# The last block's router logits, cut into bfloat16 parts and set among the first expert products

## The chip, the cores and the metric

The kernel runs on one NeuronCore of a Trainium2 chip. The metric is the device time of one execution in microseconds; less is better. Before the change it was 520.13 us, the median of 3 runs (519.86 to 521.75).

## The reference, cut to what matters

Three layers follow each other: a local-plus-summary attention, a dense layer with an ELU, and a top-1 mixture of 8 experts on 1536 tokens of width 512. The change touches only the router of the last layer and what hangs on it:

```python
logits = x @ w_gate                      # [1536, 512] @ [512, 8]
e_idx = np.argmax(logits, axis=1)
probs = np.exp(logits - logits.max(-1, keepdims=True))
probs /= probs.sum(-1, keepdims=True) + 1e-09
gate_w = probs[np.arange(N), e_idx]
eom = 1.0 / (1.0 + np.exp(-(x @ w_output_gate)))
for e in range(E):
    mask = e_idx == e
    h = np.maximum(x[mask] @ w1[e], 0.0)
    out[mask] = gate_w[mask, None] * eom[mask, e, None] * (h @ w2[e])
```

Both gates stand side by side in one matrix of 16 columns (`wg`).

## The kernel before, in words

Tokens are worked on in four blocks (512, 256, 384 and 384 tokens). For each block the kernel computes attention, then the dense layer chunk by chunk; `mm_y` ends it, `out_y1` takes a tile of 128 tokens to SBUF (tile `m`) and stores it to DRAM (`mdram`). Then the tile is transposed on TensorE (`lg_turn`) and multiplied with the gates (`lg2`). Blocks 0 to 2 do this with three bfloat16 parts of the transposed tile (`mab` holds the two upper parts, `mc` the rest) against three parts of the gates (`wg3`, 48 columns), which `lg_parts` makes in four steps: ScalarE, VectorE, ScalarE, VectorE. Block 3 copies its three tiles (`mt`) and multiplies in float32 with 16 columns.

After block 3 comes the expert layer, in slots of 128 tokens of one expert. The first two slots (0 and 1) were chosen early, from the first nine tiles alone; all other slots need the routing of all twelve tiles. So after block 3's logits a chain runs, mostly on VectorE: `route_block` (argmax and counts), the count matmul and `route_a2` (which expert owns which slot), `route_gate_*` (weights), `route_b` and `places` (place of each token), the twelve matmuls of `invert`, and `lists`, which makes `gixL` (rows to gather), `sixL` (rows to scatter to) and `sclL` (weights). With `gixL`, POOL gathers the tokens of a slot from `mdram` (`x_load`, tile `xg`, an indirect DMA); TensorE transposes them (`x_T`), and ScalarE and VectorE split them into a high and a low part (`holdh`, `holdl`). Here slots 2, 3 and 4 are the first late ones. The gather of slot i+2 is issued when slot i has been transposed. `route_a3` makes `nxi`, the experts that come next; SP waits for it and then loads the next expert's weights (`load_next`, 4 MB into `wo`). Behind those loads, in the same queue, stand the loads of the small slots' weights (`w_direct`, tiles `w2q`, `w2p`).

While the chain runs, TensorE works on slots 0 and 1: 48 products of 128 x 512 in `mm1` (tile `h`) and 48 in `mm2` (tile `y`), with four groups of transposes between (`g_T`, tile `S`). "Product" below always means one of these.

The order of the last part is written by a small planner, `second`: each step has an engine, a cost from the table `COST` and the steps it needs, and the planner picks what can start first. Engines run their lists strictly in that order. `flag` loads a slot's expert number into a register of ScalarE and VectorE, and `renew` is a branch on it: if a slot's expert is that of the slot before, nothing is converted.

Of the kernel before, what the change touches and what calls it, by code (L numbers as in the profile page):

```python
# [70 lines left out]
PB, PX = 2, 3  # L71
LF, NL = KF - 2, KF - 2 + PB + PX
NY = 2 * (PB + PX)
COST = {'m': 0.685, 'mp': 0.907, 't': 0.43, 'a': 0.48, 'l': 0.6, 'o': 0.57, 'g': 1.04, 'hAct': 0.52, 'lat': 0.08, 'xg': 2.0, 'dma': 0.73, 'pc': 0.1, 'px': 0.3, 'pg': 0.4, 'pb': 0.0, 'tol': 0.05, 'if': 0.15}
START2 = dict(PE=1.9, Act=0.9, DVE=1.4, Pool=0.5)
PARTS = range(8), range(8, 12), range(12, 16)
SEQ = (2, 3, 4, 11, 5, 6, 12, 7, 8, 9, 10)
# [4 lines left out]
class Prog:  # L82
# [499 lines left out]

    def lg_parts(self, j, t):

        nc, T = self.nc, self.mT.pop((j, t))
        if j == NBLK - 1:
            mt = self.t2k.tile([128, 512], F32, tag="t2k", name="mt")
            (nc.vector.tensor_copy if t == 1 else nc.scalar.copy)(mt, T)
        else:
            ab, c, r = (self.stg.tile([128, n, 512], dt, tag="stg", name=nm) for n, dt, nm in ((2, BF16, "mab"), (1, BF16, "mc"), (1, F32, "mr")))  # L590
            mt = [ab[:, 0], ab[:, 1], c[:, 0]]
            nc.scalar.copy(mt[0], T)
            nc.vector.tensor_tensor(r[:, 0], T, mt[0], op=ALU.subtract)
            nc.scalar.copy(mt[1], r[:, 0])
            nc.vector.tensor_tensor(mt[2], r[:, 0], mt[1], op=ALU.subtract)
        self.mt[j, t] = mt

    def lg2(self, j, t):
        nc = self.nc
        mt = self.mt.pop((j, t))  # L600
        if j < NBLK - 1:
            L = (self.bank(self.psa, "S") if j == NBLK - 2 else self.bank(self.psy, "y"))[:, :48]
            for k in range(4):
                for i in range(3):
                    nc.tensor.matmul(L, lhsT=mt[i][:, k * 128:k * 128 + 128], rhs=self.wg3[:, k], start=(k == 0 and i == 0), stop=(k == 3 and i == 2))
            nc.vector.tensor_reduce(self.lg[:, U0[j] // 2 + t], L.rearrange("p (i n) -> p n i", i=3), axis=AX.X, op=ALU.add)
            return
        if t == 0:
            self.L3 = self.bank(self.psy, "y")
        for k in range(4):  # L610
            nc.tensor.matmul(self.L3[:, t * 16:t * 16 + 16], lhsT=mt[:, k * 128:k * 128 + 128], rhs=self.wg[:, k], start=(k == 0), stop=(k == 3))

    def lg3(self):
        n = TPB[-1]
        self.nc.vector.tensor_copy(self.lg[:, NTT - n:], self.L3[:, :16 * n].rearrange("p (t e) -> p t e", t=n))

    def part1(self):
        nc = self.nc
# [212 lines left out]
    def route_gate_e(self, j):  # L831
# [2 lines left out]
        self.nc.scalar.activation(den[:, 1], z, AF.Exp, scale=-1.0)  # L834
        self.gate[j] = ex, den

    def route_gate_b(self, j):
        nc, sm = self.nc, self.small
        n = TPB[j]
        ts = slice(U0[j] // 2, U0[j + 1] // 2)  # L840
        ex, den = self.gate[j]
        nc.vector.tensor_reduce(den[:, 0], ex, axis=AX.X, op=ALU.add)
        nc.vector.tensor_scalar(den[:, 0], den[:, 0], 1e-9, None, op0=ALU.add)
        nc.vector.tensor_scalar(den[:, 1], den[:, 1], 1.0, None, op0=ALU.add)
# [65 lines left out]
    def lists(self, key, ps, n):  # L910
        nc = self.nc
        tk = self.small("f_tk" + key, [6, n])
        nc.vector.tensor_copy(tk, ps.rearrange("p (v s) -> p v s", s=n))
        ix = self.small("f_ix", [NL])[:, :n]
        nc.vector.scalar_tensor_tensor(ix, tk[:, 1], 128.0, tk[:, 0], op0=ALU.mult, op1=ALU.add)
        gix = self.const.tile([128, n], U32, name="gix" + key)
        six = self.const.tile([128, n], U32, name="six" + key)
        scl = self.const.tile([128, n], F32, name="scl" + key)
        nc.vector.tensor_copy(gix, ix)
        o = self.small("f_o", [NL])[:, :n]  # L920
        nc.vector.tensor_scalar(o, tk[:, 5], -4096.0, 4096.0, op0=ALU.mult, op1=ALU.add)
# [369 lines left out]
    def second(self, seq, t, start=False):  # L1291
# [72 lines left out]
        if start:  # L1364
            J = NBLK - 1
            for i in range(TPB[J]):
                e, d = ("DVE", C["l"]) if i == 1 else ("Act", C["a"])
                mm("c", ("yl", i), C["m"], [], lambda i=i: self.mm_y1(J, NF - 1, i))
                op(("m", i), e, d, [("yl", i)], lambda i=i: self.out_y1(J, i))
                op(("md", i), "Pool", C["g"], [("m", i)], lambda i=i: self.store_m(nc.gpsimd, J, i))  # L1370
            for i in range(TPB[J]):
                e, d = ("DVE", C["l"]) if i == 1 else ("Act", C["a"])
                mm("c", ("lt", i), C["t"], [("m", i)], lambda i=i: self.lg_turn(J, i))
                op(("mt", i), e, d, [("lt", i)], lambda i=i: self.lg_parts(J, i))
            for i in range(TPB[J]):
                mm("c", ("lg", i), 0.84, [("mt", i)], lambda i=i: self.lg2(J, i))
            op(("lv",), "DVE", 0.12, [("lg", i) for i in range(TPB[J])], self.lg3)
            op(("rb",), "DVE", 1.62, [("lv",)], lambda: self.route_block(J))
            mm("c", ("cnt",), 0.05, [("rb",)], self.count)
            mm("c", ("rm",), 0.05, [("rb",)], lambda: self.rank_mm(TE, NTT, self.fin))  # L1380
            op(("left",), "DVE", 0.1, [("cnt",)], self.left)
            op(("ga",), "DVE", 0.3, [("rb",)], lambda: self.route_gate_a(J))
            op(("ge",), "Act", 0.25, [("ga",)], lambda: self.route_gate_e(J))
            op(("a2",), "DVE", 2.75, [("left",)], self.route_a2)
            op(("rk",), "DVE", 0.35, [("rm",)], lambda: self.rank_of(TE, NTT, self.fin))
            op(("gb",), "DVE", 0.6, [("ge",)], lambda: self.route_gate_b(J))
            op(("gc",), "Pool", 1.4, [("gb",)], lambda: self.route_gate_c(J))
            op(("a4",), "DVE", 1.05, [("a2",)], self.route_a4)
            op(("b1",), "DVE", 2.3, [("a4",), ("rk",)], self.route_b)
# [12 lines left out]

            for i in range(16):
                if i < WN:
                    done["w", chain[0], i] = 0.0
                    continue
                self.ew[0, i] = self.new_place(f"wi{i}")
                op(("h0", i), "Act", C["hAct"], [], lambda i=i: self.conv_hi("Act", 0, i, self.ew[0, i]))
                op(("w", 0, i), "DVE", C["l"], [("h0", i)], lambda i=i: self.last_w(i))
        else:  # L1410
            done["xg", 0] = C["xg"]
            for i in range(16):
                done["w", chain[0], i] = C["xg"]
            half = [(0.0, p) for i in range(8) for p in self.float_places(f"wi{i}")]
# [17 lines left out]
        while any(pe.values()) or fixed:  # L1432
# [152 lines left out]
```

## Time and profile before

| What | Value |
|---|---|
| Median of 3 runs | 520.13 us |
| Profiled execution's own time | 519.82 us |
| Its span (first to last instruction) | 518.0 us |
| TensorE busy | 508.6 us, 98% |
| VectorE, ScalarE, POOL busy | 65%, 59%, 11% |
| Mean granted TensorE clock | 0.994 of full |

TensorE's busy time is modelled, so waits show better in the places where two products stand further apart than usual. The span's parts: dense layer until about 339 us, logits of block 3 until 343.7 us, slots 0 and 1 until 371.2 us, then the late slots until 512 us and a tail for the last scatter.

### The profile page before, as it was taken

The page shows a single profiled execution, that of the slowest core. Times are in us where ns is not written, and L with a number is a line of the kernel's source. Part 1 is how long each engine was busy: PE and PEld are TensorE (multiplying, and loading weights), DVE is VectorE, ACT ScalarE, POOL GpSimd, SP SyncE. Part 2 cuts the span into 40 slices and gives each one's busy share as a digit, 9 for nine tenths or more (in the row PEclk, how much of TensorE's full clock was granted, in tenths as well). Part 3 has the DMA queues.
Part 4 walks back from the last instruction along what each step waited for, and adds up shares of the span by engine and source line. Part 5 has one row for each costly group of instructions (what it writes and reads, how often), then busy time and mean ns, then how long its engine had stood idle before and what let it go on. Part 6 is the DMA issues. An engine that isn't in the chain of part 4 may idle for free. (4 is left out here: it accounts for less than half of the span.)

```text
span 518.0 us, 9835 instructions
## 1 busy us (share of the span) xinstructions
PE 508.6 (98%) x3325; PEld 408.5 (79%) x3325; DVE 336.7 (65%) x945; ACT 305.0 (59%) x715; POOL 57.2 (11%) x103
## 2 busy tenths in 40 slices
PE   8999999999999999999999999999999999999995
PEld 6486778888988889888899898888788566576884
DVE  5999999999798768776557899658321011445510
ACT  3899999986777667656546556433232222556521
POOL 3510200001000000000000001013411111100001
PEclk9999999999999999999999999989999999999998
DMA  8999444561420221200001034210599899594501
GB/s 287 404 398 317 146 133 138 183 198 50 135 77 7 83 82 42 83 15 1 2 0 63 1 126 164 78 62 1 157 339 301 292 348 360 168 364 143 213 23 44
DMA packets 37131, 78.08 MB, mean 151 GB/s; under 512 B 3951, under 2 KB 9807, under 8 KB 37072
## 3 DMA queue, kind: packets, MB, share of 16 engines
q1 hardware_dynamic: 34752, 70.02, 39.7%
q0 software_dynamic: 2320, 7.34, 4.0%
q8 instruction: 28, 0.46, 0.4%
q14 instruction: 31, 0.25, 0.2%
HBM read 100.37 MB, written 6.55 MB: 206 GB/s over the span
## 5 line engine op out<-in xcount | busy, mean ns | idle before, releaser
L483 PE MATMUL h<-xh,wi 128*128 128x384 f32 (+2 forms) x528 | 141.8, 337 | 1.5 <-DVE elp L509 1.5
L544 PE MATMUL y<-wsp,gh 128*128 128x512 f32 x368 | 116.8, 399 | 0.0
L483 PEld LDWEIGHTS h<-xh,wi 128*128 128x128 f32 x528 | 93.9, 189 | 9.4 <-DVE elp L509 1.9
L483 PE MATMUL h<-xl,wi 128*128 128x384 f32 (+2 forms) x264 | 87.5, 332 | 0.0
L544 PEld LDWEIGHTS y<-wsp,gh 128*128 128x128 f32 x368 | 66.5, 188 | 12.1 <-issue 0.3
L544 PE MATMUL y<-wsp,gl 128*128 128x512 f32 x184 | 72.4, 393 | 0.0
L1228 DVE TENSOR_TENSOR holdl<-S,holdh 128x512 fp32r<-128x512 f32 x22 | 15.2, 690 | 73.2 <-ACT holdh L1224 55.1
L1196 PE MATMUL h<-w2s,holdh 128*128 128x512 f32 x176 | 61.1, 408 | 0.0
L1239 PE MATMUL y<-w2s,holdh 128*128 128x512 f32 x176 | 59.0, 398 | 0.0
L483 PEld LDWEIGHTS h<-xl,wi 128*128 128x128 f32 x264 | 49.9, 189 | 3.8 <-issue 0.5
L503 DVE SCALAR_TENSOR_TENSOR elt<-ele,elt 128x384 f32<-128x384 f32 (+2 forms) x64 | 35.5, 554 | 24.3 <-ACT ele L496 23.9
L175 ACT CAST wsp<-wo 128x512 fp32r<-128x512 f32 x62 | 38.0, 618 | 19.9 <-PE y L544 19.1
L179 DVE TENSOR_TENSOR wsp<-wo,wsp 128x512 fp32r<-128x512 f32 x62 | 42.6, 688 | 8.3 <-ACT wsp L175 8.2
L496 ACT ACTIVATE elt<-h 128x384 f32<-128x384 f32 (+2 forms) x64 | 31.2, 487 | 25.1 <-PE h L483 24.4
L519 ACT CAST gh<-elp 128x384 fp32r<-128x384 f32 (+2 forms) x62 | 31.5, 509 | 20.9 <-DVE elp L509 13.8
L544 PEld LDWEIGHTS y<-wsp,gl 128*128 128x128 f32 x184 | 34.6, 188 | 7.9 <-DVE gl L525 0.3
L525 DVE TENSOR_TENSOR gl<-elp,gh 128x384 fp32r<-128x384 f32 (+2 forms) x62 | 34.0, 549 | 10.2 <-ACT gh L519 9.9
L1196 PEld LDWEIGHTS h<-w2s,holdh 128*128 128x128 f32 x176 | 33.7, 191 | 8.2 <-issue 0.8
L354 ACT ACTIVATE e<-e,nb 128x120 f32<-128x120 f32 x88 | 33.6, 386 | 9.8 <-DVE nb L341 9.8
L1239 PEld LDWEIGHTS y<-w2s,holdh 128*128 128x128 f32 x176 | 33.1, 188 | 6.7
L1273 DVE TENSOR_TENSOR w2s<-wo,w2s 128x512 fp32r<-128x512 f32 x48 | 30.4, 686 | 10.5 <-PE y L1239 5.5
L509 DVE SCALAR_TENSOR_TENSOR elp<-elt,h 128x384 f32<-128x384 f32 (+2 forms) x64 | 35.1, 548 | 0.8
(291 smaller groups left out, 820.4 us busy)
## 6 DMA issues: line engine op xcount, KB each, us to landing
wo<-in_w SPq DMA_DIRECT2D x9, 2048.0 KB
wo<-in_w SPq DMA_DIRECT2D x18, 1024.0 KB
ri<-in_w_in SPq DMA_DIRECT2D x16, 512.0 KB
ro<-in_w_out SPq DMA_DIRECT2D x16, 512.0 KB
wo<-in_w SPq DMA_DIRECT2D x32, 256.0 KB
w2p<-in_w SPq DMA_DIRECT2D x32, 256.0 KB
w2q<-in_w SPq DMA_DIRECT2D x24, 256.0 KB
k<-in_kw SPq DMA_DIRECT2D x18, 192.0 KB
```

Of the source, the lines that this page charges most:

```text
L175: self.nc.scalar.copy(w[:, 0], self.w[c, 1].bitcast(F32))
L179: self.nc.vector.tensor_tensor(w[:, 1], self.w[c, 1].bitcast(F32), w[:, 0].bitcast(F32), op=ALU.subtract)
L354: nc.scalar.activation(e[:, p], e[:, p], AF.Exp, bias=nb[:, p:p + 1], scale=-1.0, accum_out=sm[:, p:p + 1])
L483: nc.tensor.matmul(h, lhsT=w[:, wl, k * 128:k * 128 + 128], rhs=x[:, k, a:b], start=(n == 0), stop=(n == 11))
L496: self.nc.scalar.activation(self.te[j, c][i], self.h[j, c], AF.Exp if i else AF.Tanh, scale=1.0 if i else 0.5)
L503: nc.vector.scalar_tensor_tensor(t, e, 1.0, t, op0=ALU.add, op1=ALU.mult)
L509: nc.vector.scalar_tensor_tensor(p, t, 0.0, h, op0=ALU.min, op1=ALU.max)
L519: self.nc.scalar.copy(gh, p)
L525: self.nc.vector.tensor_tensor(gl, p, gh.bitcast(F32), op=ALU.subtract)
L544: nc.tensor.matmul(self.y[j][t], lhsT=gx[:, sl], rhs=wx, start=(c == 0 and n == 0), stop=(c == NF - 1 and n == len(ops) - 1))
L1196: nc.tensor.matmul(self.h[s, hf], lhsT=x[:, k], rhs=w, start=(n == 0), stop=(n == 11))
L1239: nc.tensor.matmul(self.y2[s], lhsT=g[:, ks], rhs=w, start=(i == 0 and n == 0), stop=(i == 7 and n == 2))
```

## The change

In block 3, tiles 0 and 1 are now cut into three bfloat16 parts as in the other blocks (in buffers of a former `x` tile: `mh`, `ml`); tile 2 stays in float32. The steps of the cutting are planned one by one (`lg_b`, `lg_c`, `lg_d`). The logits stand after the first six products, tile 2 first. Two conversions of slot 0's weights wait until the second tile `m` has been copied. Two small additions of the gate weights go from VectorE to POOL. The gathers no longer stand behind the making of `sixL` and `sclL` (`list_rest`), and `route_a3` now needs the lists and slot 1's last `holdl`, not slot 2's transposed tokens. In `COST` a gather of the first two late slots is given 3.1 us to land instead of 2.0.

```diff
-COST = {'m': 0.685, 'mp': 0.907, 't': 0.43, 'a': 0.48, 'l': 0.6, 'o': 0.57, 'g': 1.04, 'hAct': 0.52, 'lat': 0.08, 'xg': 2.0, 'dma': 0.73, 'pc': 0.1, 'px': 0.3, 'pg': 0.4, 'pb': 0.0, 'tol': 0.05, 'if': 0.15}
+COST = {'m': 0.685, 'mp': 0.907, 't': 0.43, 'a': 0.48, 'l': 0.6, 'o': 0.57, 'g': 1.04, 'hAct': 0.52, 'lat': 0.08, 'xg': 2.0, 'dma': 0.73, 'pc': 0.1, 'px': 0.3, 'pg': 0.4, 'pb': 0.0, 'tol': 0.05, 'if': 0.15, 'xf': 3.1}
...
     def lg_parts(self, j, t):
-        nc, T = self.nc, self.mT.pop((j, t))
+        if j == NBLK - 1 and t > 1:
+            self.mt[j, t] = [self.t2k.tile([128, 512], F32, tag="t2k", name="mt")], None
+            self.nc.scalar.copy(self.mt[j, t][0][0], self.mT.pop((j, t)))
+            return
         if j == NBLK - 1:
-            mt = self.t2k.tile([128, 512], F32, tag="t2k", name="mt")
-            (nc.vector.tensor_copy if t == 1 else nc.scalar.copy)(mt, T)
+            if t == 0:
+                n = TPB[j]
+                self.mab, self.mc = (self.xp.tile([128, n, 512], F32, tag=f"x{p}{j % 2}", name=f"m{p}").bitcast(BF16).rearrange("p t (i n) -> p t i n", i=2) for p in "hl")
+            mt = [self.mab[:, t, 0], self.mab[:, t, 1], self.mc[:, t, 0]]
+            r = self.t2k.tile([128, 512], F32, tag="t2k", name="mr")
...
+    def lg_b(self, j, t):
+        mt, r = self.mt[j, t]
+        self.nc.vector.tensor_tensor(r, self.mT.pop((j, t)), mt[0], op=ALU.subtract)
+
+    def lg_c(self, j, t):
+        mt, r = self.mt[j, t]
+        self.nc.scalar.copy(mt[1], r)
+
+    def lg_d(self, j, t):
+        mt, r = self.mt[j, t]
+        self.nc.vector.tensor_tensor(mt[2], r, mt[1], op=ALU.subtract)
...
+    def lg3a(self):
+        self.nc.vector.tensor_copy(self.lg[:, NTT - 1], self.L3[:, 96:112])
     def lg3(self):
-        n = TPB[-1]
-        self.nc.vector.tensor_copy(self.lg[:, NTT - n:], self.L3[:, :16 * n].rearrange("p (t e) -> p t e", t=n))
+        self.nc.vector.tensor_reduce(self.lg[:, NTT - 3:NTT - 1], self.L3[:, :96].rearrange("p (t i e) -> p t e i", t=2, i=3), axis=AX.X, op=ALU.add)
...
+    def route_gate_d(self, j):
+        den = self.gate[j][1]
+        eng = self.nc.gpsimd if j == NBLK - 1 else self.nc.vector
+        eng.tensor_scalar(den[:, 0], den[:, 0], 1e-9, None, op0=ALU.add)
+        eng.tensor_scalar(den[:, 1], den[:, 1], 1.0, None, op0=ALU.add)
...
         nc.vector.tensor_copy(gix, ix)
+        if key == "L":
+            self.rest = lambda: self.list_rest(tk, ix, n, six, scl)
+        else:
+            self.list_rest(tk, ix, n, six, scl)
+        return gix, six, scl
...
-            op(("li",), "DVE", 1.4, [("inv",)], lambda: setattr(self, "L_", self.lists("L", self.slots_of(), NL)))
+            op(("li",), "DVE", 0.65, [("inv",)], lambda: setattr(self, "L_", self.lists("L", self.slots_of(), NL)))
             for i in (2, 3):
                 op(("xg", i), "Pool", C["g"], [("li",)], lambda i=i: self.x_load(seq[i]))
+            op(("lj",), "DVE", 0.9, [("on", "xg", 2)], lambda: self.rest())
             op(("f", 2), "Act", 0.46, [("li",)], lambda: self.flag(2))
-            op(("a3",), "DVE", 1.6, [("xl", 2)], self.route_a3)
+            op(("a3",), "DVE", 1.6, [("lj",), ("gl", 1, 1)], self.route_a3)
...
-                op(("w", 0, i), "DVE", C["l"], [("h0", i)], lambda i=i: self.last_w(i))
+                op(("w", 0, i), "DVE", C["l"], [("h0", i)] + ([("m", 1)] if i > 13 else []), lambda i=i: self.last_w(i))
```

TensorE, from the transposes of block 3 on, before the change:

```order
L580 MATMUL T<-c_162,m 128x128 x4
L580 MATMUL S<-c_162,m 128x128 x4
L580 MATMUL y<-c_162,m 128x128 x4
L611 MATMUL y<-rc,mt 128x16 x12
L1196 MATMUL h<-w2s,holdh_4461 128x512
L1196 MATMUL h<-w2s,holdl_4462 128x512
```

The same place after the change (`c` is the identity, `rc` and `wg` the gates in float32 and in parts):

```order
L580 MATMUL y<-c_162,m 128x128 x4
L1239 MATMUL h<-w2s,holdh_4461 128x512
L1239 MATMUL h<-w2s,holdl_4462 128x512
L1239 MATMUL h<-w2s,holdh_4461 128x512 x2
L1239 MATMUL h<-w2s,holdl_4462 128x512
L1239 MATMUL h<-w2s,holdh_4461 128x512
L627 MATMUL y<-rc,mt 128x16 x4
L633 LDWEIGHTS mh
L633 MATMUL y<-wg_1005,mh 128x48
```

Six products now stand before the logits; of the twelve float32 matmuls four are left, and 24 short ones with 48 columns follow.

VectorE, the rows up to `nxi`, before the change (the first row is the split of slot 2's tokens, the others are `route_a3`):

```order
L1180 TENSOR_TENSOR holdl_4462<-T,holdh_4461 128x512
L1028 TENSOR_SCALAR f_e_4976<-f_en 128x8
L1031 TENSOR_TENSOR mask<-rc,f_e_4976 128x72
L1032 SCALAR_TENSOR_TENSOR mask<-mask,f_e_4976 128x72
L1034 TENSOR_REDUCE f_to<-mask 128x9
L1035 TENSOR_TENSOR mask<-f_to,f_e_4976 128x72
L1036 TENSOR_REDUCE f_to<-mask 128x9
L1038 TENSOR_SCALAR nxi<-f_to,e_1029 128x9
L1039 TENSOR_SCALAR nxi<-nxi 128x9
```

The same step after the change:

```order
L1071 TENSOR_SCALAR f_e_4978<-f_en 128x8
L1074 TENSOR_TENSOR mask<-rc,f_e_4978 128x72
L1075 SCALAR_TENSOR_TENSOR mask<-mask,f_e_4978 128x72
L1077 TENSOR_REDUCE f_to<-mask 128x9
L1078 TENSOR_TENSOR mask<-f_to,f_e_4978 128x72
L1079 TENSOR_REDUCE f_to<-mask 128x9
L1081 TENSOR_SCALAR nxi<-f_to,e_1029 128x9
L1082 TENSOR_SCALAR nxi<-nxi 128x9
L1223 TENSOR_TENSOR holdl_4462<-T,holdh_4461 128x512
```

`nxi` now stands ahead of the split of slot 2's tokens and no longer behind it.

TensorE where the late slots' tokens are transposed, before the change (slots 3 and 4, then slot 2's first products):

```order
L1171 MATMUL T<-identr,xg 128x128 x4
L1239 MATMUL y<-w2s,holdh_4838 128x512
L1239 MATMUL y<-w2s,holdl_4839 128x512
L1239 MATMUL y<-w2s,holdh_4838 128x512 x2
L1239 MATMUL y<-w2s,holdl_4839 128x512
L1239 MATMUL y<-w2s,holdh_4838 128x512 x2
L1239 MATMUL y<-w2s,holdl_4839 128x512
L1239 MATMUL y<-w2s,holdh_4838 128x512
L1171 MATMUL T<-identr,xg 128x128 x4
L1282 UNCONDITIONAL_BRANCH
L1196 MATMUL h<-w2s,holdh_4461 128x512
```

And after it:

```order
L1214 MATMUL T<-identr,xg 128x128 x4
L1325 UNCONDITIONAL_BRANCH
L1239 MATMUL h<-w2s,holdh_4461 128x512
L1239 MATMUL h<-w2s,holdl_4462 128x512
L1239 MATMUL h<-w2s,holdh_4461 128x512 x2
L1239 MATMUL h<-w2s,holdl_4462 128x512
L1239 MATMUL h<-w2s,holdh_4461 128x512 x2
L1239 MATMUL h<-w2s,holdl_4462 128x512
L1239 MATMUL h<-w2s,holdh_4461 128x512
L1325 UNCONDITIONAL_BRANCH x2
L1214 MATMUL T<-identr,xg 128x128 x4
L1239 MATMUL h<-w2s,holdh_4461 128x512
```

The transposes of slots 2, 3 and 4 each stand nine products later than before, with the same nine between one and the next; slot 4's now come after nine of slot 2's own products.

## Rows read from the trace of the kernel before

**Rows 1.** Part 1 of the page: busy time, share, instructions of each engine.

```profile
PE 508.6 (98%) x3325; PEld 408.5 (79%) x3325; DVE 336.7 (65%) x945; ACT 305.0 (59%) x715; POOL 57.2 (11%) x103
```

**Rows 2.** Windows of one us: busy per engine, then clock, DMA share, GB/s.

```profile
344.00:345.00 1.00, 1.00 (x4) 0.77 (x4) 0.86 (x5) 0.22 (x1) 0.00 (x0) 0.69 0.04 12
345.00:346.00 1.00, 1.00 (x4) 0.76 (x3) 0.83 (x6) 0.00 (x0) 0.00 (x0) 0.50 0.00 0
346.00:347.00 1.00, 1.00 (x4) 0.56 (x2) 0.11 (x1) 0.21 (x1) 0.00 (x0) 0.50 0.00 0
347.00:348.00 1.00, 1.00 (x6) 0.77 (x6) 0.45 (x4) 0.00 (x0) 0.00 (x0) 0.61 0.00 0
```

**Rows 3.** Timeline 341 to 344: start, length, engine, line, tiles, shapes [idle before].

```profile
341.14 2.75 PE L611 MATMUL y<-rc,mt 128*128 128x16 f32 x24
...
343.74 0.48 PE L1196 MATMUL h<-w2s,holdh 128*128 128x512 f32 x1
```

**Rows 4.** Timeline of TensorE, 144 to 146: block 0's logits by parts.

```profile
144.92 0.22 PE L605 MATMUL y<-wg,mab 128*128 128x48 bf16 x2
...
145.23 0.36 PE L483 MATMUL h<-xh,wi 128*128 128x256 f32 x1
```

**Rows 5.** Groups by line, 136 to 222: busy us, mean ns | idle before.

```profile
L593 DVE TENSOR_TENSOR mr<-y,mab 128x512 f32<-128x512 f32 x6 | 4.1, 686 | 0.0
...
L594 ACT CAST mab<-mr 128x512 bf16<-128x512 f32 x6 | 3.7, 622 | 1.9 <-DVE mr L593 1.9
```

**Rows 6.** Timeline 347 to 363: the routing chain, from the counts to the gather.

```profile
347.52 0.16 DVE L996 SCALAR_TENSOR_TENSOR e_c<-taken,y 128x8 f32<-128x8 f32 x1 [1.41 <-PE y L880]
...
350.90 0.18 DVE L842 TENSOR_REDUCE r_den<-r_ex 128x3 f32<-128x24 f32 x1 [0.19 <-ACTq L1282]
...
359.95 0.50 PEld L908 LDWEIGHTS <-A 128*128 128x128 bf16 x12 [0.26 <-DVE v L902]
...
361.12 0.17 DVE L919 CAST gixL<-f_ix 128x14 uint32<-128x14 f32 x1
...
361.90 0.17 DVE L925 TENSOR_TENSOR sclL<-sclL,f_tkL 128x14 f32<-128x14 f32 x1
...
362.06 1.09 POOL L1157 DMA_INDIRECT xg<-mdram,gixL  x1 [4.05 <-PE y L1239]
```

**Rows 7.** Timeline 361.9 to 371.5: products, gathers, transposes of slots 2 to 4.

```profile
361.95 0.39 PE L1239 MATMUL y<-w2s,holdl 128*128 128x512 f32 x1
...
362.64 0.39 PE L1239 MATMUL y<-w2s,holdl 128*128 128x512 f32 x1
...
365.60 0.39 PE L1239 MATMUL y<-w2s,holdh 128*128 128x512 f32 x1
...
366.23 0.53 PE L1171 MATMUL T<-identr,xg 128*128 128x128 f32 x4 [0.24 <-DMA xg<-mdram,gixL]
...
367.03 0.98 POOL L1157 DMA_INDIRECT xg<-mdram,gixL  x1 [0.38 <-DMA xg<-mdram,gixL]
...
367.42 0.69 DVE L1180 TENSOR_TENSOR holdl<-T,holdh 128x512 fp32r<-128x512 f32 x1 [4.48 <-ACT holdh L1176]
...
369.82 0.17 DVE L1039 TENSOR_SCALAR nxi<-nxi 128x9 int32<-128x9 int32 x1
...
371.01 13.88 SPq L1499 DMA_DIRECT2D wo<-in_w  x5
...
371.16 0.46 PE L1171 MATMUL T<-identr,xg 128*128 128x128 f32 x4
...
371.42 0.33 DVE L1065 TENSOR_TENSOR mask<-rc,f_T 128x160 f32<-128x160 f32 x1 [0.83 <-DVEq L1282]
```

**Rows 8.** DMA issues: gathers issued at 367.03, 371.89, 380.24; last, us to landing.

```profile
xg<-mdram,gixL POOLq DMA_INDIRECT x1, 3.4
...
xg<-mdram,gixL POOLq DMA_INDIRECT x1, 7.8
...
xg<-mdram,gixL POOLq DMA_INDIRECT x1, 6.9
```

**Rows 9.** Waits of TensorE's weight loads from 340 on: total us, times, longest.

```profile
PEld h L1205 <- DMA w2p<-in_w: 0.6, 2, 0.3
```

More of the change, by code (lines that the diff above doesn't have):

```diff
@@ L591, in lg_parts @@
             mt = [ab[:, 0], ab[:, 1], c[:, 0]]
[L592 to L596, printed above, removed]
+            r = r[:, 0]
+        self.mt[j, t] = mt, r
+        self.nc.scalar.copy(mt[0], self.mT[j, t])
+        if j < NBLK - 1:
+            self.lg_b(j, t)
+            self.lg_c(j, t)
+            self.lg_d(j, t)
@@ L598, in lg2 @@
+    def lg_b(self, j, t):
[7 more added lines that the diff above has]
+        self.nc.vector.tensor_tensor(mt[2], r, mt[1], op=ALU.subtract)
     def lg2(self, j, t):
         nc = self.nc
-        mt = self.mt.pop((j, t))
+        mt = self.mt.pop((j, t))[0]
+        if j == NBLK - 1:
+            if t == 2:
+                self.L3 = self.bank(self.psy, "y")
+            L = self.L3[:, t * 48:t * 48 + 48]
+            if t > 1:
+                for k in range(4):
+                    nc.tensor.matmul(L[:, :16], lhsT=mt[0][:, k * 128:k * 128 + 128], rhs=self.wg[:, k], start=(k == 0), stop=(k == 3))
+                return
+        else:
+            L = (self.bank(self.psa, "S") if j == NBLK - 2 else self.bank(self.psy, "y"))[:, :48]
+        for k in range(4):
+            for i in range(3):
+                nc.tensor.matmul(L, lhsT=mt[i][:, k * 128:k * 128 + 128], rhs=self.wg3[:, k], start=(k == 0 and i == 0), stop=(k == 3 and i == 2))
@@ L601, in lg2 @@
         if j < NBLK - 1:
[L602 to L605, printed above, removed]
             nc.vector.tensor_reduce(self.lg[:, U0[j] // 2 + t], L.rearrange("p (i n) -> p n i", i=3), axis=AX.X, op=ALU.add)
-            return
-        if t == 0:
-            self.L3 = self.bank(self.psy, "y")
@@ L610, in lg2 @@
-        for k in range(4):
-            nc.tensor.matmul(self.L3[:, t * 16:t * 16 + 16], lhsT=mt[:, k * 128:k * 128 + 128], rhs=self.wg[:, k], start=(k == 0), stop=(k == 3))
+    def lg3a(self):
+        self.nc.vector.tensor_copy(self.lg[:, NTT - 1], self.L3[:, 96:112])
     def lg3(self):
-        n = TPB[-1]
-        self.nc.vector.tensor_copy(self.lg[:, NTT - n:], self.L3[:, :16 * n].rearrange("p (t e) -> p t e", t=n))
+        self.nc.vector.tensor_reduce(self.lg[:, NTT - 3:NTT - 1], self.L3[:, :96].rearrange("p (t i e) -> p t e i", t=2, i=3), axis=AX.X, op=ALU.add)
@@ L835, in route_gate_e, with route_gate_z @@
         self.gate[j] = ex, den
+    def route_gate_z(self, j):
+        ex, den = self.gate[j]
+        self.nc.vector.tensor_reduce(den[:, 0], ex, axis=AX.X, op=ALU.add)
+    def route_gate_d(self, j):
[3 more added lines that the diff above has]
+        eng.tensor_scalar(den[:, 1], den[:, 1], 1.0, None, op0=ALU.add)
     def route_gate_b(self, j):
@@ L840, in route_gate_b @@
         ts = slice(U0[j] // 2, U0[j + 1] // 2)
[L841 to L844, printed above, removed]
+        if j < NBLK - 1:
+            self.route_gate_z(j)
+            self.route_gate_d(j)
+        den = self.gate[j][1]
         nc.vector.reciprocal(den, den)
@@ L919, in lists, with list_rest @@
         nc.vector.tensor_copy(gix, ix)
+        if key == "L":
+            self.rest = lambda: self.list_rest(tk, ix, n, six, scl)
+        else:
+            self.list_rest(tk, ix, n, six, scl)
+        return gix, six, scl
+    def list_rest(self, tk, ix, n, six, scl):
+        nc = self.nc
         o = self.small("f_o", [NL])[:, :n]
@@ L925, in lists @@
         nc.vector.tensor_tensor(scl, scl, tk[:, 4], op=ALU.add)
-        return gix, six, scl
     def route_early(self):
@@ L1373, in second @@
                 mm("c", ("lt", i), C["t"], [("m", i)], lambda i=i: self.lg_turn(J, i))
[L1374 to L1377, printed above, removed]
+                op(("ma", i), "Act", C["a"], [("lt", i)], lambda i=i: self.lg_parts(J, i))
+                if i == 2:
+                    continue
+                op(("mb", i), "DVE", C["l"], [("ma", i)], lambda i=i: self.lg_b(J, i))
+                op(("mc", i), "Act", C["a"], [("mb", i)], lambda i=i: self.lg_c(J, i))
+                op(("mt", i), "DVE", C["l"], [("mc", i)], lambda i=i: self.lg_d(J, i))
+            mm("c", ("lg", 2), 0.9, [("ma", 2)], lambda: self.lg2(J, 2))
+            for i in range(2):
+                mm("c", ("lg", i), 0.34, [("mt", i)], lambda i=i: self.lg2(J, i))
+            op(("la",), "DVE", 0.2, [("lg", 2)], self.lg3a)
+            op(("lv",), "DVE", 0.25, [("lg", 0), ("lg", 1), ("la",)], self.lg3)
             op(("rb",), "DVE", 1.62, [("lv",)], lambda: self.route_block(J))
@@ L1385, in second @@
             op(("rk",), "DVE", 0.35, [("rm",)], lambda: self.rank_of(TE, NTT, self.fin))
-            op(("gb",), "DVE", 0.6, [("ge",)], lambda: self.route_gate_b(J))
+            op(("gz",), "DVE", 0.2, [("ge",)], lambda: self.route_gate_z(J))
+            op(("gd",), "Pool", 0.45, [("gz",)], lambda: self.route_gate_d(J))
+            op(("gb",), "DVE", 0.2, [("gd",)], lambda: self.route_gate_b(J))
             op(("gc",), "Pool", 1.4, [("gb",)], lambda: self.route_gate_c(J))
             op(("a4",), "DVE", 1.05, [("a2",)], self.route_a4)
-            op(("b1",), "DVE", 2.3, [("a4",), ("rk",)], self.route_b)
+            op(("b1",), "DVE", 2.3, [("a4",), ("rk",), ("gl", 0, 0)], self.route_b)
             op(("pp",), "Pool", 0.58 * (NTT - PD), [("b1",)], lambda: self.places(nc.gpsimd, PD, NTT))
@@ L1473, in second @@
                 o[4]()
-                done[o[0]] = end + (C["xg"] if o[0][0] == "xg" else 0.0)
+                done[o[0]] = end + ((C["xf"] if start and o[0][1] < 4 else C["xg"]) if o[0][0] == "xg" else 0.0)
+                done[("on",) + o[0]] = st
                 if o[0][0] == "ld":
```

## The prediction

> **What bounds the kernel now.** I read the page first: TensorE is busy for 98% of the span [rows 1], so a change counts only where it shortens TensorE's list, ends a wait of TensorE, or makes a new one. Then I read the granted clock in windows of one microsecond: over the whole span until TensorE's last product it falls only once, to its lower level (1.2 GHz), from about 344.4 to 347.8 [rows 2]. What stood just before are the 24 passes of block 3's float32 logits, 16 columns each [rows 3]. The missing shares of those four windows, 0.31 + 0.50 + 0.50 + 0.39, are 1.70 us lost. Then I followed the timeline of the routing chain to slot 2's tokens [rows 6, 7], because it sets when TensorE's next work is there. TensorE waits in it twice: for VectorE at the twelve matmuls of `invert` (0.26 us) [rows 6], and for the gather at slot 2's transposes. There the last product starts at 365.60, the transposes at 366.23; a product takes 0.23 us (three start within 0.69) [rows 7], so 0.40 us of the step is wait. From there on TensorE waits for next to nothing; the only transfer that it is seen waiting for is `w2p`, 0.6 us [rows 9].
>
> **The change, part by part.** Times are those of the profiled execution (span 518.0, own time 519.82, which is 0.31 under the median of 520.13).
>
> *Logits.* Before, they fill TensorE from 341.14 to 343.74, 2.60 us, 0.108 per pass [rows 3]. After, 8 passes (four matmuls of tile 2) are left, 0.87 us. The 24 short matmuls I price by block 0, where twelve of them stand between 144.92 and 145.23 [rows 4]: 0.31 us for twelve, 0.62 for 24. The parts of tile 1 are ready late: two conversions, then four subtractions of 0.69 and two casts of 0.62 [rows 5] end at about 343.8 by my count, and the last twelve matmuls could start at 343.7, so 0.1 us is waited. Sum 1.6 us instead of 2.6: **−1.0**. The six products set ahead cover the cutting; without them about 1.4 us of it would be bare.
>
> *The clock.* The 2.6 us of small work become 1.6 us with 1.4 us of full products ahead of them. No row of before shows this mixture, so the price lies between 0 (it falls as before) and −1.70 (it doesn't). The nearest row is that of block 0, where twelve such short matmuls lie between full products and the clock stays at its upper level; I take **−1.70**.
>
> *The chain.* The logits end 0.4 us later (344.1 for 343.7), but the count matmul, which stood behind nine slow products (VectorE waited 1.41 us for it [rows 6]), now stands 12 products of full speed behind the logits: 344.1 + 2.8 = 346.9, and VectorE goes on some 0.3 us later, at 347.2 instead of 347.52. The sum and the two additions of the gate weights (the first takes 0.18 at 350.90 [rows 6]) leave the path, about −0.5. So `invert` could start at 359.95 − 0.3 − 0.5 = 359.15. TensorE, 2.7 us ahead and with six more products (1.4 us) to do before it, gets there at 358.4 and waits 0.7 us where it waited 0.26: **+0.4**.
>
> *Lists and gather.* Before, the gather starts at 362.06, 0.77 us after `gixL` (361.12 + 0.17) and close to the end of `sclL` at 362.07 [rows 6]. If it waited for the later lists, it now comes up to 0.5 us sooner; if not, nothing changes. Either way it is issued by about 361.3 and lands 4.1 us later as before, at 365.4; slot 2's transposes, 9 products later in the list, come at 365.7. So the old wait goes: **−0.4**.
>
> Up to slot 2's first product that is −2.7: 368.4 instead of 371.16 (slot 4's transposes apart, which stood ahead of it).
>
> *The new wait.* `nxi` waited for the split of slot 2's tokens at 367.42 and was ready at 369.99; SP then issued 4 MB of weights from 371.01 [rows 7]. Now `nxi` follows the lists: `invert` at 359.15, then 1.34 to `gixL`, 0.78 for the later lists, one register load and one branch (two branches and a load took 0.83 [rows 7]; 0.6 here), a split of 0.69 and `route_a3`, 1.9 (368.11 to 369.99): about 364.5. SP issues 1.0 us later, at 365.5, 5.5 us earlier than before. The gather for slot 4 can't follow: it is issued 0.8 us after slot 2's transposes (367.03 − 366.23 [rows 7]), now 365.7 + 0.8 = 366.5, so 1.0 us *behind* the weights, where it was 4.0 us ahead. Gathers issued before the weights land after 3.4 us; the one issued 0.88 us behind them, at 371.89, took 7.8, and one in the middle of them 6.9 [rows 8]. TensorE takes slot 4's tokens 4.93 us after slot 2's (371.16 − 366.23 [rows 7]; the list has the same nine products between each), now at 370.6. A gather of 3.4 lands at 369.9, in time; one of 6.9 to 7.8 lands at 373.4 to 374.3, and TensorE, strictly in order, stands for 2.8 to 3.7 us. Behind these transposes stand all of slot 2's later products. Between 0 and 3.7 I take **+3.0**, near the lower of the two crowded rows, since less of the stream is under way by then.
>
> Here a page speaks for the change. The Trainium skill (DMA: Bandwidth & Descriptors, section Queues, rings and completion order) says that each DMA engine takes turns between the queues that have work, packet by packet, so a gather from POOL's queue would lose little to SP's loads. The rows of 6.9 and 7.8 beside 3.4 don't bear that out for this kernel; by that rule the wait would be near 0 and the sum near −3.2.
>
> *Earlier weights.* The small slots' weights stand in SP's queue behind those 4 MB and come about 5 us earlier, so the wait for `w2p` goes: **−0.5** of the 0.6, at best −0.6 and at worst 0.
>
> *Rest.* POOL's two additions (each some 0.2) end long before VectorE's reciprocal; the delayed conversions of slot 0 are needed by its second layer's end, ten microseconds later. Behind slot 4's transposes the list of TensorE is the same as before. These cost nothing.
>
> Sum: −1.0 − 1.7 + 0.4 − 0.4 + 3.0 − 0.5 = −0.2, that is 519.6 for the profiled execution, **519.8** on the median. Most of what the logits give is taken back 26 us later by one gather.
>
> **The rivals.**
> *The gather slips through.* It lands in 3.4 us, because `nxi` is later than I count (2 us would surely do) or because the queues take turns. Then the +3.0 is 0: 519.8 − 3.0 = 516.8. For it: the rows have nothing between a gather 4.0 us ahead of the weights, untouched, and one 0.88 us behind them, crowded, so the border may lie close. Against: the order counted above, with 1.0 us on the wrong side.
> *The standing TensorE loses its clock.* In the wait of some 3 us TensorE has nothing at all, and 2.6 us of small work were enough to end at the lower level before. If it falls once more at the same price, +1.7: 521.5, slower than before. It decides from a wait of about the length of that small work on, so only where the crowded gather takes 6.9 us or more. Against: half a product group still stands on either side. The Trainium skill (TensorE: Matmul & The Clock Gate, section HAM oscillation) says likewise that waits for a transfer between bursts of matmuls can return the engine to its lower clock; the trace of before has no such wait to show it.
> *The clock falls at the logits as before,* so that the short matmuls among the products don't do for the clock what I count on. TensorE loses 1.7 us, the count comes 1.35 us later, the wait at `invert` shrinks by 0.35 and all after it shifts by 1.35; the gather is as crowded as in the main case. 519.8 + 1.3 = 521.1.
>
> **How the numbers follow.** My forecast (gather crowded, clock kept) 0.45; the gather slips through 0.21; the second fall 0.20; the first fall stays 0.14. The likeliest time is 519.8, its own range 518.8 to 520.6. Over all cases I give 516.8 to 522.0. A difference of 0.5% (2.6 us) is about what a measurement of this kernel can tell from no change, so "faster" means under 517.5: nearly only the gather that slips through, 0.20 with a little from the main case. "Slower" means over 522.7: both falls together or a longer wait, 0.11. The rest, 0.69, is no change.
>
> **What would show it.** Right: four float32 matmuls and 24 short ones after six products, done by 344.2; a clock at its upper level from 344 to 348; `nxi` near 364.5 and SP's first load of weights near 365.5; the gather for slot 4 landing after 6 us or more; a gap of TensorE of about 3 us before slot 4's transposes; no wait for `w2p`. Wrong: a clock of 0.5 in 344 to 348 (logits), `nxi` after 366 or a gather of 3.4 us (no gap), or a clock of 0.5 shortly after 371 (second fall). If slot 2's first product comes later than 369.5, my count of the chain has failed.

## The result and the profile after

The changed kernel takes **525.24 us** (median of 5 runs, 525.09 to 525.40), the kernel before 520.13 (5 runs, 519.29 to 521.75): ratio 1.0091, 95% interval 1.0070 to 1.0112. It is slower by 0.9%; 519.8 was forecast, with a range up to 522.0.

The logits first. The timeline of TensorE answers to [rows 3], the one-us windows (busy per engine, then clock, DMA share, GB/s) to [rows 2]:

```profile
340.51 0.60 PE L580 MATMUL T<-c,m 128*128 128x128 f32 x4
...
343.23 0.96 PE L627 MATMUL y<-rc,mt 128*128 128x16 f32 x8
344.04 0.21 PE L633 MATMUL y<-wg,mh 128*128 128x48 bf16 x2
...
344.76 0.21 PE L633 MATMUL y<-wg,mh 128*128 128x48 bf16 x2 [0.26 <-DVE lg L638]
...
345.06 0.47 PE L1239 MATMUL h<-w2s,holdh 128*128 128x512 f32 x1
```

```profile
345.00:346.00 1.00, 1.00 (x13) 0.87 (x10) 0.64 (x4) 0.00 (x0) 0.00 (x0) 1.00 0.04 16
346.00:347.00 1.00, 1.00 (x7) 0.79 (x6) 0.85 (x5) 0.22 (x1) 0.00 (x0) 1.00 0.00 0
347.00:348.00 1.00, 1.00 (x9) 0.66 (x7) 0.61 (x4) 0.70 (x3) 0.20 (x1) 1.00 0.00 0
```

Logits by parts and the clock came as counted: no fall, and from block 3's first transposes to the next product 4.55 us, of which the six products take 1.37 (0.2275 each). That leaves 3.18 for 4.05 before (339.69 to 343.74).

Six microseconds later is a wait that the forecast doesn't have. TensorE and VectorE, timeline:

```profile
350.09 0.39 PE L1239 MATMUL h<-w2s,holdl 128*128 128x512 f32 x1
351.51 0.73 PE L1239 MATMUL h<-w2s,holdh 128*128 128x512 f32 x2 [1.04 <-DVEq L1325]
```

```profile
350.92 0.23 DVE L1061 TENSOR_SCALAR esi<-f_es,e 128x9 int32<-128x9 f32 x1
351.18 0.17 DVE L1062 TENSOR_SCALAR esi<-esi 128x9 int32<-128x9 int32 x1
351.55 0.19 DVE L881 RECIPROCAL r_den<-r_den 128x6 f32<-128x6 f32 x1 [0.19 <-DVEq L1325]
```

Line 1325 is the branch of `renew` for slot 1. VectorE comes to it only after all of `route_a2`, whose last operations make `esi`. Behind the branch VectorE would write the low part of slot 1's weights, and the first product that reads a low part is slot 1's third, the 27th of all. It waits for the branch and starts 1.42 us after the 26th, 1.19 more than a product takes. Before the change (VectorE's last operation ahead of the branch, then TensorE's 26th and 27th products):

```profile
350.54 0.17 DVE L1019 TENSOR_SCALAR esi<-esi 128x9 int32<-128x9 int32 x1
...
351.71 0.39 PE L1196 MATMUL h<-w2s,holdl 128*128 128x512 f32 x1
351.94 0.62 PE L1196 MATMUL h<-w2s,holdh 128*128 128x512 f32 x2
```

Counted from block 3's first transposes, VectorE came to the branch about as early as now (10.85 us then, 10.67 now), but TensorE came to the 27th product later, 12.25 us after the transposes, and waited for nothing.

Then the weights, the gather and the gap, answering to [rows 7, 8]. First the timeline, then the gather's DMA row (last: us to landing), then windows:

```profile
366.16 0.17 DVE L1082 TENSOR_SCALAR nxi<-nxi 128x9 int32<-128x9 int32 x1
...
367.35 0.41 SPq L1553 DMA_DIRECT2D wo<-in_w  x1
...
368.25 0.97 POOL L1200 DMA_INDIRECT xg<-mdram,gixL  x1 [1.44 <-DMA xg<-mdram,gixL]
...
372.13 0.39 PE L1239 MATMUL h<-w2s,holdh 128*128 128x512 f32 x1
376.85 0.56 PE L1214 MATMUL T<-identr,xg 128*128 128x128 f32 x4 [4.33 <-DMA xg<-mdram,gixL]
```

```profile
xg<-mdram,gixL POOLq DMA_INDIRECT x1, 8.5
```

```profile
376.00:377.00 1.00, 0.15 (x2) 0.18 (x3) 0.00 (x0) 0.00 (x0) 0.00 (x0) 1.00 1.04 410
377.00:378.00 1.00, 1.00 (x6) 0.90 (x6) 0.00 (x0) 0.00 (x0) 0.32 (x1) 0.59 1.03 408
378.00:379.00 1.00, 1.00 (x3) 0.75 (x3) 0.00 (x0) 0.09 (x1) 0.65 (x1) 0.50 1.03 401
379.00:380.00 1.00, 1.00 (x4) 0.77 (x3) 0.00 (x0) 0.51 (x1) 0.00 (x0) 0.50 1.06 408
380.00:381.00 1.00, 1.00 (x5) 0.78 (x4) 0.00 (x0) 0.00 (x0) 0.00 (x0) 0.71 1.06 408
```

The gather was issued 0.90 us behind the first load of weights and took 8.5 us. TensorE stood 4.33 us, and just after the stand its clock fell: 0.41 + 0.50 + 0.50 + 0.29 = 1.70 us lost.

For the experiments I use a ruler that no wait earlier in the program touches: from block 3's first transposes to the last product. Identical work ahead of it ends between 339.09 and 340.63 in the eleven profiles of this study, so 0.82 of the difference of 5.42 between the two profiled executions (525.24 and 519.82) has nothing to do with the change. The last product before and after:

```profile
511.79 0.39 PE L1239 MATMUL y<-w2s,holdh 128*128 128x512 f32 x1
```

```profile
517.07 0.39 PE L1282 MATMUL y<-w2s,holdh 128*128 128x512 f32 x1
```

Before: 511.79 − 339.69 = 172.10. After: 517.07 − 340.51 = 176.56.

| Kernel | Ruler, us | Median, us | Before beside it | Ratio (95% interval) |
|---|---|---|---|---|
| changed | 176.56 | 525.24 | 520.13 | 1.0091 (1.0070 to 1.0112) |
| 1 weights behind the gather | 171.72 | 520.17 | 519.16 | 1.0019 (1.0002 to 1.0036) |
| 2 before, early weights | 178.00 | 524.96 | 519.16 | 1.0098 (1.0072 to 1.0125) |
| 3 busy wait | 175.48 | 523.71 | 519.16 | 1.0081 (1.0056 to 1.0106) |
| 4 slot 4's tokens planned late | 170.92 | 519.62 | 519.16 | 1.0001 (0.9987 to 1.0016) |
| 5 as 4, branch early | 169.62 | 517.49 | 519.65 | 0.9962 (0.9948 to 0.9977) |
| 6 as 4, float32 logits | 174.21 | 521.93 | 519.65 | 1.0052 (1.0032 to 1.0073) |
| 7 as 5, count early | 169.15 | 517.14 | 519.65 | 0.9956 (0.9937 to 0.9975) |
| 8 as 7, copy after the logits | 169.08 | 517.37 | 519.30 | 0.9964 (0.9951 to 0.9976) |
| 9 changed, branch early only | 172.87 | 522.18 | 519.30 | 1.0050 (1.0031 to 1.0069) |

### The profile page after: what moved, and what is told of

It is laid out like the page before. It is cut to its first block, busy times and chain, and to the rows that moved or that the text cites. A ratio compares the mean times of both kernels' runs of the same rounds, so it can differ in the third digit from the quotient of the medians.

```text
span 523.5 us, 9855 instructions
## 1 busy us (share of the span) xinstructions
PE 507.0 (97%) x3333; PEld 406.7 (78%) x3333; DVE 339.5 (65%) x947; ACT 306.5 (59%) x718; POOL 57.4 (11%) x105
```

## The experiments

**1. The weights behind the gather again.**

```diff
-op(("a3",), "DVE", 1.6, [("lj",), ("gl", 1, 1)], self.route_a3)
+op(("a3",), "DVE", 1.6, [("lj",), ("gl", 1, 1), ("xl", 2)], self.route_a3)
```

> The changed kernel, but `route_a3` (which makes `nxi`) needs slot 2's split tokens again, as before the change. Theory A (the 4 MB of weights, issued 0.9 us ahead of slot 4's gather, stretch it to 8.5 us; TensorE stands 4.3 us for it and then loses its clock for 1.7): SP issues the weights about 4 us behind the gather, the gather lands after 3.4 to 4 us, no gap and no second fall: 525.2 - 4.3 - 1.7 = 519.2 us (518.6 to 519.8). Rival B (the gather is slow because of the scatter issued before it in POOL's own queue): the gather still takes more than 6 us, 523 us or more.

520.17 us, 1 us above the expectation and outside its range. The gap and the fall are gone (mean clock 0.996 to 0.999 in its twelve runs), so the weights made them and not the scatter ahead of the gather. Timeline (POOL's gather, ScalarE, TensorE, SP's weights):

```profile
366.83 0.97 POOL L1200 DMA_INDIRECT xg<-mdram,gixL  x1 [1.44 <-PE T L1214]
...
369.37 0.58 ACT L1219 CAST holdh<-T 128x512 fp32r<-128x512 f32 x1
...
370.04 0.50 PE L1239 MATMUL h<-w2s,holdh 128*128 128x512 f32 x1 [1.07 <-ACTq L1325]
...
371.54 0.46 PE L1214 MATMUL T<-identr,xg 128*128 128x128 f32 x4
...
371.97 16.11 SPq L1553 DMA_DIRECT2D wo<-in_w  x6
```

The weights come 5.1 us behind the gather, and slot 4's transposes, 4.7 us behind it, wait for nothing. But TensorE stands 1.07 us before slot 2's first product, again for a branch. Here the line names ScalarE's, which in this order stands behind slot 3's `holdh` (done at 369.95). VectorE's branch, now behind `route_a3`, was passed 0.15 us before ScalarE's. This second branch wait is about what the expectation missed.

**2. The early weights alone, in the kernel before.**

```diff
-op(("a3",), "DVE", 1.6, [("xl", 2)], self.route_a3)
+op(("a3",), "DVE", 1.6, [("li",), ("gl", 1, 1)], self.route_a3)
```

> The kernel before, with one edit: `route_a3` needs only the lists and slot 1's last `holdl`. Logits stay in float32. Theory A: `nxi` near 365, weights issued near 366, about 1 us ahead of slot 4's gather (367.0), which then takes some 8 us; TensorE stands about 3.9 us before slot 4's transposes and loses its clock for 1.7: 520.1 + 3.9 + 1.7 = 525.7 us (524.5 to 526.5), although the clock falls at the logits too. Rival B (the weights are innocent): 520.1 us, no gap.

524.96 us: theory A. One dependency is enough for the whole loss. The wait, and windows of one us behind it and at its float32 logits:

```profile
374.97 0.72 PE L1171 MATMUL T<-identr,xg 128*128 128x128 f32 x4 [4.66 <-DMA xg<-mdram,gixL]
```

```profile
346.00:347.00 1.00, 1.00 (x8) 0.64 (x8) 0.82 (x7) 0.21 (x1) 0.00 (x0) 1.00 0.00 0
...
376.00:377.00 1.00, 1.00 (x4) 0.76 (x3) 0.00 (x0) 0.00 (x0) 0.91 (x1) 0.50 1.05 389
```

The clock fell while TensorE still stood (0.50 in each window from 374 to 380, 0.62 in the next). From the end of the stand on this cost 2.9 us and not the 1.7 that was expected; the profiled run is the slowest of the six (526.43). The clock did *not* fall at the logits (1.00 at 346), although these are the old float32 logits. I come back to that below.

**3. The same wait with TensorE busy.** Nineteen products fill it:

```diff
 T = self.tx[s] = self.bank(self.psa, "T")
+if s == 4:
+    for _ in range(19):
+        nc.tensor.matmul(T, lhsT=self.xs[2][0][:, 0], rhs=self.ew[2, 0][0], start=True, stop=True)
```

> The changed kernel, with 19 more products of 128 x 512 (slot 2's first one repeated, into a bank that the transposes overwrite) just before slot 4's transposes, 4.3 us of work in a wait of 4.3 us. Theory A (the clock falls because TensorE stands): the gather still lands at the same time, the clock stays at its upper level behind it: 525.2 - 1.7 = 523.5 us (523.2 to 524.2). Rival C (the second fall comes from the transposes and branches around that place, or would come anyway): it falls as before, 525.2 us or a little more.

523.71 us. Timeline, the gather's DMA row, and a window behind:

```profile
372.56 4.61 PE L1215 MATMUL T<-w2s,holdh 128*128 128x512 f32 x19 [0.39 <-DVE holdl L1226]
377.01 0.46 PE L1217 MATMUL T<-identr,xg 128*128 128x128 f32 x4
```

```profile
xg<-mdram,gixL POOLq DMA_INDIRECT x1, 8.7
```

```profile
378.00:379.00 1.00, 1.00 (x7) 0.80 (x6) 0.00 (x0) 0.60 (x1) 0.71 (x1) 1.00 1.04 397
```

The gather is as late as before (8.7), the useful work resumes no sooner (36.88 us after block 3's first transposes, 36.34 in the changed kernel), and yet the kernel gains 1.5 us (525.24 to 523.71; 1.08 on the ruler), because the clock stays. The two medians come from different sessions and the intervals of their ratios overlap; what carries the reading is the clock, at its upper level behind the transposes in this trace and 0.996 to 0.999 on the mean in all six runs. So the stand costs its clock on top of its length. The Trainium skill (TensorE: Matmul & The Clock Gate, section HAM oscillation) says that waits for a transfer between bursts of matmuls can bring the lower clock; these runs agree.

**4. Early weights kept, slot 4's tokens planned late.** The planner is told what the crowded gather takes:

```diff
-done[o[0]] = end + ((C["xf"] if start and o[0][1] < 4 else C["xg"]) if o[0][0] == "xg" else 0.0)
+done[o[0]] = end + ((C["xf"] if start and o[0][1] < 4 else 9.0 if start and o[0][1] == 4 else C["xg"]) if o[0][0] == "xg" else 0.0)
```

> The changed kernel, with the planner told that slot 4's gather takes 9 us to land: its transposes move some 24 products (5.5 us) further back in TensorE's list; the weights stay early. Theory A: the gather still takes 7 to 8.5 us, but TensorE has products to do meanwhile: no gap, no second fall, 519.2 us (518.3 to 520). If the wait only moves (slot 3 or 5 then stand for theirs), 521 us or more. Rival B makes no difference here.

519.62 us, as expected: the gather still takes 8.0 us, nobody waits for it, and the mean clock is 0.997 to 0.999 in all twelve runs. But this removes 4.33 + 1.70 and lands where the kernel before is. The 2.7 us of the logits and their clock must have gone elsewhere. The trace shows the same 1.04 us in front of slot 1's third product (351.11, released by VectorE's branch). Experiments 5 and 6 ask for the rest.

**5. The branch earlier in VectorE's list.** The last four operations of `route_a2` move to `route_a6`, behind the lists:

```diff
-op(("a2",), "DVE", 2.75, [("left",)], self.route_a2)
+op(("a2",), "DVE", 1.95, [("left",)], self.route_a2)
...
-op(("f", 2), "Act", 0.46, [("li",)], lambda: self.flag(2))
+op(("a6",), "DVE", 0.8, [("lj",)], self.route_a6)
+op(("f", 2), "Act", 0.46, [("li",), ("a6",)], lambda: self.flag(2))
```

> The kernel of the late-planned tokens (slot 4's gather planned at 9 us), and the last four operations of `route_a2`, which make `esi` (0.97 us of VectorE), move out of it to behind the lists, so that the branch of `renew` for slot 1 stands 0.97 us earlier in VectorE's list. Theory D (TensorE stands 1.4 us at slot 1's first product because this product follows a branch that VectorE reaches only after its routing): the gap between the two products around that branch shrinks from 1.4 to about 0.4, the chain behind the branch comes 0.9 earlier, and the time falls by 0.9: 519.6 - 0.9 = 518.7 us; from block 3's first transposes to the last product 170.0 us for 170.9. Rival E (TensorE's lead is only handed on: it stands at `invert` or for slot 2's gather instead): the gap shrinks but the sum stays, 519.6 us and 170.9.

517.49 us, ratio 0.9962: faster than both kernels. Around the branch:

```profile
349.41 0.39 PE L1243 MATMUL h<-w2s,holdl 128*128 128x512 f32 x1
349.83 0.73 PE L1243 MATMUL h<-w2s,holdh 128*128 128x512 f32 x2
```

0.42 from product to product where it was 1.42 to 1.43, as theory D said (the expectation calls it slot 1's first product; it is the third). The ruler is 1.30 shorter (0.9 expected): 0.90 of it is there at slot 2's first product, the other 0.40 comes after it. Rival E fell: the lead isn't lost again at `invert` or at the gather. What made the 0.40 is not shown. The edit also moved the weights: they are now issued 0.29 us behind slot 4's gather (366.16, 365.87), as in experiment 9.

**6. The float32 logits back, everything else as in 4.**

```diff
-if j == NBLK - 1 and t > 1:
+if j == NBLK - 1:
...
-op(("mb", i), "DVE", C["l"], [("ma", i)], lambda i=i: self.lg_b(J, i))
-op(("mc", i), "Act", C["a"], [("mb", i)], lambda i=i: self.lg_c(J, i))
-op(("mt", i), "DVE", C["l"], [("mc", i)], lambda i=i: self.lg_d(J, i))
```

> The kernel of the late-planned tokens with the float32 logits of before put back: three copied tiles and twelve float32 matmuls, at the same place behind six products; no parts, everything else in the same order. Theory D (clock and parts are worth what TensorE doesn't give back by standing at slot 1's branch): the clock falls behind the logits as before, 1.7 us lost, logits 0.7 us later; the count stands 12 products behind them, so VectorE's chain is late by both and nothing is given back at the branch: about +2.3, 521.9 us, and 173.2 us from block 3's first transposes to the last product. Rival F (the six products ahead are enough to keep the clock): no fall, +0.7, 520.3 us. Rival G (the 1.7 us come back as a shorter wait at the branch): 520.3 us as well, but with a clock that falls.

521.93 us, as theory D said. Timeline and window:

```profile
344.85 1.07 PE L627 MATMUL y<-rc,mt 128*128 128x16 f32 x8 [0.27 <-DVE lg L638]
...
353.82 0.73 PE L1239 MATMUL h<-w2s,holdh 128*128 128x512 f32 x2 [1.07 <-DVEq L1325]
```

```profile
347.00:348.00 1.00, 1.00 (x4) 0.73 (x3) 0.83 (x7) 0.00 (x0) 0.00 (x0) 0.50 0.00 0
```

In the profiled run six products ahead of the float32 logits don't keep the clock, and nothing comes back at the branch, because the count matmul is late by the same amount: rival G falls. Rival F falls only in part: four of the six runs have a mean granted clock of 0.993 (521.6 to 523.4 us), two have 0.996 and 0.997 and take 521.1 and 521.3, still more than F's 520.3. On the ruler the parts are worth 174.21 − 170.92 = 3.29 us in this execution, 1.0 more than expected: the products resume 1.20 us later and not 0.7, and 0.5 come after slot 2's first product, for a reason that no run shows. On the medians it is 2.3. So what the logits promised was there; the rest of the change hid it.

**9. The branch alone, in the changed kernel** (the edit of 5 without that of 4).

> The changed kernel with one edit: `esi` is made behind the lists, so that the branch of `renew` for slot 1 comes earlier. The early weights and the crowded gather of slot 4 stay. Theory A and D: the wait at the branch goes (1.3 us, as it did in the kernel of the late-planned tokens), all steps behind it, `nxi`, the weights and the gather, come earlier by the same, so the gap before slot 4's transposes and the second fall stay as long: 525.2 - 1.3 = 523.9 us. Rival J (TensorE's lead only makes its wait for the gather longer): 525.2 us.

522.18 us, 1.7 below the expectation. Timeline (SP's first load, the gather, TensorE) and a window behind the stand:

```profile
366.22 0.98 POOL L1204 DMA_INDIRECT xg<-mdram,gixL  x1 [0.70 <-PE T L1218]
...
366.52 0.41 SPq L1558 DMA_DIRECT2D wo<-in_w  x1
...
373.70 0.51 PE L1218 MATMUL T<-identr,xg 128*128 128x128 f32 x4 [3.21 <-DMA xg<-mdram,gixL]
```

```profile
374.00:375.00 1.00, 1.00 (x7) 0.87 (x6) 0.00 (x0) 0.00 (x0) 0.51 (x1) 1.00 0.96 315
```

I had left out that `nxi` now stands behind `esi`: the weights come 0.30 us *behind* the gather. It is still crowded (7.3 us), but TensorE stands only 3.21 us, and in this execution (521.08) the clock stays. In most other runs of this kernel the mean clock is lower, as the last section says.

**7 and 8. The count three products earlier, and the copy of tile 2's logits behind the others.**

```diff
-op(("rb",), "DVE", 1.62, [("lv",)], lambda: self.route_block(J))
+op(("rb",), "DVE", 1.0, [("lv",)], lambda: self.route_block(J))
```

> As the kernel with the early branch, and the planner is told 1.0 us for `route_block` instead of 1.62: the count matmul stands three products earlier in TensorE's list, where VectorE waited 0.47 us for it. Theory D: the chain and with it the rest of the wait at the branch come 0.4 us earlier, 518.3 us; 169.6 us from block 3's first transposes to the last product. Rival E: no change against the kernel with the early branch.

```diff
-op(("la",), "DVE", 0.2, [("lg", 2)], self.lg3a)
+op(("la",), "DVE", 0.2, [("lg", 2), ("lg", 1)], self.lg3a)
```

> As the kernel with the early count, but the copy of tile 2's logits (`lg3a`, which reads the PSUM bank that the other two tiles' logits go to) is planned behind the last logits instead of between tile 0's and tile 1's. Theory H (TensorE's 0.27 us of wait before tile 1's logits, seen also where no parts were made, is a wait for that copy to leave the bank): the wait goes, TensorE's products resume 0.2 to 0.45 us earlier after the transposes, VectorE does the copy 0.2 later: 517.0 us, no change in the time that shows. Rival I (the wait is for the parts of tile 1): it stays.

7 gives 517.14 us and a ruler 0.47 shorter than 5, as expected, though the medians alone (517.49, 517.14) can't tell the two apart. In 8 the wait for the copy goes, TensorE resumes 0.15 us sooner (4.41 after the first transposes instead of 4.56), less than the 0.2 to 0.45 expected, and the time stays (517.37). So the copy was about half of the 0.27 (theory H); the rest is the parts of tile 1, whose last one is ready only at 344.60 in this trace (rival I). Kernels 5, 7 and 8 beat both the kernel before and the changed one.

## Why the prediction was wrong

**The new wait was seen and sized too small.** Place, order and cause were right: `nxi` early, weights 1.0 us ahead of the gather (0.90 in the trace), TensorE standing before slot 4's transposes. `nxi` (366.33) and the gather (368.25) both came nearly 2 us later than counted, 0.82 of it from ahead of the logits and the rest from the chain (below); the order between them held because both were late together. But the step "I take +3.0, near the lower of the two crowded rows, since less of the stream is under way by then" failed: the gather took 8.5, more than either row of [rows 8], and the stand was 4.33. Nothing in the trace spoke for the lower end: the step would have had to take the row of a gather 0.88 us behind the weights (7.8, a stand of 3.7) and to allow for more.

**The second fall was the rival with 0.20, and it came.** The main sum had it at 0. In the profiled run it cost 1.70, exactly the price that the rival had; only its chance was wrong. The other four runs of the changed kernel have the same mean granted clock (0.992 to 0.994), so it was most likely there too: experiments 1, 3, 4, 5, 7 and 8 have the same logits and no such stand, and none of their 60 runs is under 0.996. Experiment 3 shows that the standing is the cause. Wait and clock came together here (a stand of 4.33 us with the lower mean clock in five of five runs, one of 3.21 in five of seven), and I priced them as if they were independent.

**The chain was followed to `invert` and not to the branch.** My count had TensorE meet VectorE at `invert` (+0.4) and nowhere before. In fact it meets it at slot 1's branch, after 26 products. What TensorE won at the clock it waited there: +1.19. The wait at `invert` went (−0.26). Slot 2's first product came at 370.23, beyond the 369.5 that I had named as the sign of a failed count. Without the 0.82 that was there before the logits it would be 369.41, just inside; the count still failed, since 1.75 us were won up to there and not 2.7. Experiment 5 settles it.

**The other terms.** Logits −0.87 (−1.0 forecast; TensorE stood 0.26 before tile 1's logits where 0.1 was counted, and experiment 8 takes 0.15 of that back by moving the copy). Clock at the logits −1.70 in the profiled execution, as forecast. Slot 2's gather −0.40, as forecast: TensorE no longer waits there, though the gather starts 0.77 us after `gixL` is done, as before. The wait for `w2p` didn't go: 0.6 before, 0.7 after for `w2p` and `pad` together, where −0.5 was forecast.

In numbers, on the two profiled executions: −0.87 − 1.70 + 1.19 − 0.26 − 0.40 is −2.04 up to slot 2's first product (the two starts give −1.75, taken from block 3's transposes); + 4.33 + 1.70 + 0.1 make +4.1 to +4.4, and the ruler says +4.46.

Set against the forecast's terms, the stand was 1.33 over its +3.0, the second fall 1.70 over nothing, the chain 0.53 over its +0.4 (1.19 − 0.26 = 0.93), the wait for the small slots' weights 0.6 over its −0.5 and the logits 0.13 over their −1.0: 4.3 of the 5.4 us between 519.8 and 525.24. The later start of block 3's transposes is 0.82 more, and the last 0.3 have no place. (The forecast's 519.6 and the 0.31 between profiled run and median make 519.9, not 519.8.)

**A size that the median doesn't carry.** The clock fall at the float32 logits isn't in every execution: experiment 2's trace has none. Of the 58 runs of the kernel before that stood beside experiments, 24 have a mean granted clock under 0.9955 (median 520.24 us) and 34 have one above (518.75). I had one profiled execution, with the fall, and took it for all. If the lower mean clock is this fall in all 24 (none of these runs has a trace), it is worth some 0.6 on many runs together (24/58 of the 1.5 between the groups) rather than 1.70.

## What to carry to other kernels

When an issue moves ahead of another queue's, ask who is just behind it: one dependency here put 4 MB of weights 0.9 us ahead of a gather of 128 rows and cost 5 us, more than the whole rest of the change could win; either order the issue behind the small transfer or plan its reader for the crowded landing time. Follow an engine that has become faster to every place where it meets the slow chain, branches included, not only to the one where it waited before. And price a long stand of TensorE together with the clock that it may cost.

## What the runs showed of the hardware that was not expected

- A gather of 128 rows lands after 3.4 us when it is issued 4.0 or 1.55 us ahead of the 1 to 2 MB loads (kernel before, issued at 367.03 and 369.46), but after 7.3 at 0.30 us ahead (experiment 9) and 0.29 us ahead (experiment 5); slot 4's gather, 0.2 to 1.1 us behind them, takes 8.0 to 8.7 (seven profiles). The Trainium skill (DMA: Bandwidth & Descriptors, section Queues, rings and completion order) lets the queues take turns packet by packet; the gather loses more here than such turns suggest, and the measurement decides. What the changed kernel's trace shows is a late start: the gather was issued at 368.25, but from 369 to 372 all packets (399, 0.82 MB) are of SP's queue, and only from 373 to 374 do the two queues share the DMA engines by halves (POOL's 51.1%, SP's 50.4%). Why POOL's packets start so late is not shown.
- A stand of 4.33 us was followed by the lower clock in the profiled run of the changed kernel, and the mean clock is as low in all five. With one of 3.21 us (experiment 9, the profiled run) it stayed; five of that kernel's seven runs have 0.993 or 0.994 and take 521.7 to 522.6 us, two have 0.996 or 0.997 and take 520.5 and 521.1. The same kernel can go either way from run to run, as at the float32 logits.
